# The last attention group in two halves, a seventh buffer of exponentials, two kinds of small work moved between VectorE and GpSimd, and a new order for all of it

## The chip, the cores and the metric

The kernel runs on one core of one Trainium2 chip. The metric is device microseconds (us) from the first to the last instruction, with some 1.7 us that the profiled span leaves out. Each run below was compared with the kernel before on the same chip, in the same rounds. The sets of runs (s1 to s4, s5 to s7, s8 to s11, s12) stood on four chips, so kernels of different sets are compared only through their ratios to the kernel before. One program gives times some 0.3% apart from run to run, and sometimes more.

## The reference, cut to what matters

```python
def reference(A_x, A_wqkv, A_wo, B_x, B_w1, B_w2, B_w3, B_w4):
    def _A_ref(x, wqkv, wo):                       # 2048 rows, 640 columns, 32 heads of 20
        ...
        scores = jnp.einsum("bhqd,bhkd->bhqk", q, k) * (Dh ** -0.5)
        p = _softmax(scores, axis=-1)
        o = jnp.einsum("bhqk,bhkd->bhqd", p, v)
        return ... @ wo
    def _B_ref(x, w1, w2, w3, w4):                 # layernorm, gelu, shifts, two MLP stages
        ...
    xn = _layernorm(A_x)
    s = _A_ref(xn, A_wqkv, A_wo)
    g = _silu(_B_ref(xn, B_w1, B_w2, B_w3, B_w4))
    return A_x + s * g
```

The attention needs 32 x 2048 x 2048 exponentials, and they set the time.

## The kernel before

Heads are worked on four at a time, queries 512 at a time: 8 x 4 = 32 groups of 16 key tiles. For two heads and one key tile TensorE makes a 128 x 1024 tile of scores in PSUM, ScalarE takes its exponential into one of six buffers, and TensorE multiplies the buffer with the values into one accumulator bank. Some key tiles go to VectorE instead, which makes their exponentials out of integer operations: an eviction (`fnu`) and "bit pieces". The second branch of the reference (B) is spread between as filler.

```python
    def exp_act(self, hs, sa):
        ...
        self.T("act", c_act(1024),
               lambda e: e.activation(self.PT[:, hp.slot, :], self.psum[...], AF.Exp, scale=cfg.scale),
               reads=[sa], writes=[pa], name=f"exp{self.step}", ..., acq=("PT", hp), rel=hs)
```

At the end of a group VectorE copies the accumulator out, so that the next group may use the bank. The sums of the exponentials go through memory and come back as reciprocals, spread over partitions; then one product finishes the group.

```python
        T("dve", c_dve(512), lambda e: e.tensor_copy(Ob[:, :], self.bank(self.PVB)[:, :]), ...)      # the copy
        ...                                                       # sums to memory and back, reciprocal
        T("sp", C_SP, lambda e: e.dma_start(RB[:, :], ...), ...)  # reciprocals, spread
        T("dve", c_dve(512, "1x"), lambda e: e.tensor_tensor(dst, Ob[:, :], RB[:, :], op=ALU.mult), ...)   # the product
```

`T` does not issue an instruction; it hands one to a planner inside the program. From assumed durations and a table of due times (`DUE`) the planner fixes, before the launch, the order in which each engine works its instructions off. On the chip every engine keeps to that order: when the next instruction's data are late, the engine stands.

## Time and profile before

| | before |
|---|---|
| time, median of 3 runs | 886.55 us |
| span of the profiled run | 884.1 us |
| first exponential | 35.65 us |
| exponentials on ScalarE | 834 |
| gaps of ScalarE from the first to the last exponential | 13.0 us |
| from the end of the last exponential to the end of the span | 11.0 us |
| busy: ScalarE, TensorE, VectorE | 96%, 93%, 81% |

The span is read as a sum along ScalarE: the start, the exponentials at 0.933 us each, 46.5 us of other functions, the gaps, the tail. The lines are in the prediction.

### The profile page before, as it was taken

What the parts mean: (1) busy time and instruction counts of PE and PEld (TensorE: products, weight loads), DVE (VectorE), ACT (ScalarE), POOL (GpSimd) and SP (SyncE); (2) the same over time, 40 slices, a digit from 0 to 9 for tenths busy, and PEclk for the clock granted to TensorE, in tenths of its full rate; (3) what the DMA queues carried; (4) which work ended last, traced back from release to release, by engine and by line L of the source; (5) the groups of instructions that cost most, each with busy time, mean ns of one, the idle gap of its engine ahead of it and who ended that gap; (6) DMA issues with size and microseconds to landing.
All of it is one profiled execution on the core that took longest, in us unless ns stands there. A gap on an engine that the chain in (4) does not pass through costs nothing.

```text
span 884.1 us, 34138 instructions
## 1 busy us (share of the span) xinstructions
PE 822.8 (93%) x15594; PEld 361.9 (41%) x15594; DVE 716.2 (81%) x986; ACT 846.9 (96%) x896; POOL 42.9 (5%) x74
## 2 busy tenths in 40 slices
PE   3899999998999999999999899999999799999996
PEld 2433333333444443433334444443433344444553
DVE  7747797876888889999998657997889794898675
ACT  7799999998999999999999999999999999999994
POOL 9500000000000000000000000000000000010000
PEclk9999999999999999999999999999999999999998
DMA  6002632331210002332122302132221212023322
GB/s 224 10 8 61 137 96 73 95 95 36 52 41 25 26 25 64 90 101 52 47 55 62 113 26 56 54 91 69 56 64 44 70 32 69 24 65 101 114 69 75
DMA packets 86481, 59.01 MB, mean 67 GB/s; under 512 B 53057, under 2 KB 77841, under 8 KB 86337
## 3 DMA queue, kind: packets, MB, share of 16 engines
q1 hardware_dynamic: 86336, 56.82, 23.5%
q8 instruction: 123, 2.02, 0.9%
q14 instruction: 22, 0.17, 0.1%
HBM read 42.10 MB, written 10.63 MB: 60 GB/s over the span
## 4 chain that ended last, share of the span: by engine, by line
ACT 55%; PE 19%; DVE 17%; DMA 5%; POOL 1%; issue 1%; POOLq 0%
ACT arena L1444 53%; PE psum L782 8%; PE psum L1420 6%; DVE arena L1371 5%; DVE arena L1471 4%; DMA arena<-recips 3%; PE psum L1345 2%; PE psum L1388 2%; DMA recips<-arena 2%; PE psum L1380 1%; ACT arena L1809 1%; DVE arena L984 1%; ACT arena L1825 1%; DVE arena L1805 1%; DVE arena L1225 1%
## 5 line engine op out<-in xcount | busy, mean ns | idle before, releaser
L1444 ACT ACTIVATE arena<-psum 128x1024 bf16<-128x1024 f32 x834 | 777.8, 1038 | 14.4 <-PE psum L1420 5.0
L1420 PE MATMUL psum<-arena 128*32 128x512 bf16 x4928 | 375.7, 381 | 8.0 <-ACT arena L1444 6.6
L782 PE MATMUL psum<-arena 128*32 128x320 bf16 (+1 forms) x5952 | 359.8, 333 | 6.8 <-DVE arena L1179 2.8
L1471 DVE TENSOR_SCALAR arena<-psum 128x1024 uint16<-128x1024 f32 (+1 forms) x192 | 231.5, 1206 | 42.1 <-PE psum L1388 41.3
L1371 DVE TENSOR_SCALAR arena<-arena 128x4096 uint16<-128x4096 uint16 (+1 forms) x224 | 231.4, 1059 | 3.6 <-PE psum L1380 2.5
L782 PEld LDWEIGHTS psum<-arena 128*32 128x32 bf16 x5952 | 150.5, 97 | 146.2 <-issue 20.7
L1345 PE MATMUL psum<-arena 128*22 128x512 bf16 x1668 | 161.8, 381 | 1.2 <-DVE arena L1506 0.6
L1420 PEld LDWEIGHTS psum<-arena 128*32 128x32 bf16 x4928 | 104.4, 95 | 137.2 <-ACT arena L1444 95.2
L1380 PE MATMUL psum<-arena 128*22 128x512 bf16 x1520 | 126.5, 380 | 2.5 <-DVE arena L1371 2.2
L1388 PE MATMUL psum<-arena 32*128 32x512 bf16 x816 | 85.4, 384 | 16.6 <-ACT arena L1444 9.7
L1345 PEld LDWEIGHTS psum<-arena 128*22 128x22 bf16 x1668 | 42.5, 92 | 55.8 <-issue 11.8
L1388 PEld LDWEIGHTS psum<-arena 32*128 32x128 bf16 x816 | 21.9, 90 | 102.5 <-ACT arena L1444 81.4
L1380 PEld LDWEIGHTS psum<-arena 128*22 128x22 bf16 x1520 | 35.8, 91 | 44.5 <-issue 9.7
L1805 DVE CAST arena<-psum 128x512 bf16<-128x512 f32 x48 | 32.8, 684 | 8.3 <-PE psum L782 8.1
L1225 DVE CAST arena<-psum 128x512 bf16<-128x512 f32 x40 | 27.3, 682 | 10.9 <-PE psum L782 10.8
L1820 DVE TENSOR_TENSOR arena<-psum,arena 128x320 bf16<-128x320 f32 x32 | 15.6, 486 | 22.0 <-PE psum L782 22.0
L1590 DVE SCALAR_TENSOR_TENSOR arena<-psum,arena 128x320 bf16<-128x320 f32 x32 | 15.6, 489 | 19.0 <-PE psum L782 18.9
L1519 DVE TENSOR_TENSOR arena<-arena 128x512 bf16<-128x512 f32 x28 | 19.2, 686 | 11.5 <-DMA arena<-recips 11.4
L984 DVE BATCH_NORM_STATS2 arena<-arena 128x6 f32<-128x320 bf16 x52 | 23.0, 480 | 2.2 <-DMA arena<-in_A_x_dram 2.2
L1286 DVE CAST arena<-psum 128x320 bf16<-128x320 f32 x32 | 15.4, 488 | 10.9 <-PE psum L782 10.5
L1506 DVE COPY arena<-psum 128x512 f32<-128x512 f32 x28 | 19.2, 685 | 3.5 <-PE psum L1345 2.3
L1089 PE MATMUL psum<-arena 128*32 128x128 bf16 x320 | 8.9, 248 | 13.7 <-DVE arena L999 13.1
(103 smaller groups left out, 283.8 us busy)
## 6 DMA issues: line engine op xcount, KB each, us to landing
arena<-in_B_w_dram SPq DMA_DIRECT2D x48, 160.0 KB, 2.6
arena<-recips SPq DMA_DIRECT2D x28, 256.0 KB
arena<-arena SPq DMA_DIRECT2D x124, 32.0 KB, 1.9
arena<-in_B_w_dram SPq DMA_DIRECT2D x4, 960.0 KB, 6.0
arena<-in_A_x_dram SPq DMA_DIRECT2D x8, 320.0 KB, 5.3
arena<-in_A_x_dram SPq DMA_DIRECT2D x16, 160.0 KB, 2.3
out_dram<-arena SPq DMA_DIRECT2D x16, 160.0 KB, 1.8
heads<-arena SPq DMA_DIRECT2D x112, 20.0 KB
```

The costliest lines, as they stand in the source:

```text
L782: ins = e.matmul(pb[32 * c:32 * c + 32, 0:N], lhsT(k, c), rhs(k, c), start=(k == 0), stop=(stop and k == nk - 1), tile_position=(0, 32 * c))
L984: lambda e, li=li, n=n, hh=hh: e.bn_stats(st[:, li, 6 * hh:6 * hh + 6], xn[:, n, hD * hh:hD * hh + hD]),
L1225: T("dve", c_dve(512), lambda e, h=h, c=c: e.tensor_copy(KS[:, 512 * c:512 * c + 512], self.wbank(h)[:, 0:512]), reads=[wa], writes=[A("KS ...
L1345: ins = e.matmul(pb[32 * i:32 * i + 22, 0:512], VA[:, ql, kts[x // 2], i, :], PT[:, slots[x // 2][0].slot, 512 * (x % 2):512 * (x % 2) + 512],
L1371: T("dve", c_dve(w, "4x"), lambda e, v=v, dst=dst: e.tensor_scalar(dst, U[:, ub, 0:w], 0.5, EXP_B[v], op0=ALU.mult, op1=ALU.add), reads=ha ...
L1380: ins = e.matmul(pb[32 * i:32 * i + 22, 0:512], wv, dst[:, at:at + 512].bitcast(BF16), start=first, stop=final, tile_position=(0, 32 * i))
L1388: return e.matmul(out, self.KT[32 * i:32 * i + 32, b, 128 * kt:128 * kt + 128], self.QT[32 * i:32 * i + 32, b, 512 * qc:512 * qc + 512], s ...
L1420: ins = e.matmul(out[32 * c:32 * c + 32, :], self.KT[:, b, 128 * kt + 32 * c:128 * kt + 32 * c + 32], self.QM[:, gb, 2 * a + jj, :], start ...
L1444: lambda e: e.activation(self.PT[:, hp.slot, :], self.psum[:, 512 * hs.slot:512 * hs.slot + 1024], AF.Exp, scale=cfg.scale),
L1471: ins = e.tensor_scalar(U[:, ub, 1024 * at + 512 * k:1024 * at + 512 * k + w], self.psum[:, 512 * hd.slots[k]:512 * hd.slots[k] + w], a_ex ...
L1506: T("dve", c_dve(512), lambda e: e.tensor_copy(Ob[:, :], self.bank(self.PVB)[:, :]), writes=[("PV", 0), A("Ob")], name=f"ob{quad}_{qc}", c ...
L1805: T("dve", c_dve(512), lambda e, h=h, fc=fc, i=i: e.tensor_copy(GT[:, i, fc, :], self.wbank(h)[:, 0:512]), reads=[wa], writes=at, name=f"g ...
```

## The change

The change means to shorten three of these terms. The last group is cut into two halves of 256 queries, so that the first half can be finished beside the second. A seventh buffer lets ScalarE run further ahead of TensorE; it is paid for with one of the seven buffers (`RR`) of branch B. The product goes to GpSimd, so that VectorE no longer waits for the reciprocals, and three clears go from GpSimd to VectorE. With these the table of due times, the number of key tiles for VectorE in each group and the assumed time of several operations were searched anew, and four normalisations left GpSimd.

```diff
-            k0=100.3, k1=-164.3, k2=-87.4, k3=-108.7, k4=-66.2, v0=-24.5, v0s=-0.38, ...
+            k0=-95.4, k1=-178.8, k2=-94.5, k3=-123.5, k4=-127.1, v0=-33.6, v0s=-0.77, ...
...
-        self.POOLN = [1, 9, 13, 15]
+        self.POOLN = []
...
+        self.ONP = 1
+        self.LAST = [[[4, 1]], []]
         self.ND = (
...
-            pl.pool("PT", 6)
+            pl.pool("PT", 7)
...
-        T("pool", 3000, lambda e: e.memset(self.QM[:, :, :, :], 0.0), ...)
+        T("dve", c_dve(4096, "4x"), lambda e: e.memset(self.QM[:, :, :, :], 0.0), ..., due=-40000.0)
...   (the same for KT and QT)
+            if last and qc == NQC - 1:
+                for half in range(2):
+                    self.last_half(quad, qc, half, gb)
...   (last_half: 256 queries, an accumulator of its own)
-        T("dve", c_dve(512, "1x"), lambda e: e.tensor_tensor(dst, Ob[:, :], RB[:, :], op=ALU.mult),
+        T("pool" if cfg.ONP else "dve", 1500 if cfg.ONP else c_dve(512, "1x"), lambda e: e.tensor_tensor(dst, Ob[:, :], RB[:, :], op=ALU.mult),
...
-        self.RR = self.alloc("RR", [7, 512], FP32)
+        self.RR = self.alloc("RR", [6, 512], FP32)
```

## The prediction

> **What bounds the kernel now.** I read the page first (shares of the span), then the groups of instructions by shape, then ScalarE's own timeline over the whole span, then the waits, and last the start and the end row by row. The page gives ACT 96%, PE 93%, DVE 81%, Pool 5%. ScalarE's work is almost all one group:
>
> ```profile
> L1444 ACT ACTIVATE arena<-psum 128x1024 bf16<-128x1024 f32 x834 | 777.8, 1038 | 14.4 <-PE psum L1420 5.0
> ...
> L1519 DVE TENSOR_TENSOR arena<-arena 128x512 bf16<-128x512 f32 x28 | 19.2, 686 | 11.5 <-DMA arena<-recips 11.4
> ```
>
> 834 exponentials took 777.8 us, so one costs 0.933 us of pace (its record of 1038 ns overlaps the next). The second row is the product that the change moves: 19.2 us of work, and 11.4 us in which VectorE stood still until the reciprocals had come back by DMA.
>
> ScalarE's timeline cuts the span in three. First, 35.65 us until the first exponential. Then 837.4 us up to the end of the last one at about 873.06: 777.8 of exponentials, 46.5 of other functions and table loads (Gelu 8.74 + 2 x 10.44, six loads of 1.28, eight Tanh at a pace of 1.15), and 13.0 of gaps, added up from the bracketed idle times. Last, 11.0 us of tail. So time goes by the count of exponentials, the gaps and the two ends. The largest gaps, in ScalarE's timeline, with the VectorE rows of the same moments from VectorE's timeline:
>
> ```profile
> 207.21 0.69 DVE L1519 TENSOR_TENSOR arena<-arena 128x512 bf16<-128x512 f32 x1 [2.86 <-DMA arena<-recips]
> ...
> 209.62 1.02 ACT L1444 ACTIVATE arena<-psum 128x1024 bf16<-128x1024 f32 x1 [2.18 <-PE psum L1388]
> ...
> 452.74 29.18 ACT L1444 ACTIVATE arena<-psum 128x1024 bf16<-128x1024 f32 x31 [1.79 <-PE psum L1345]
> ...
> 565.19 0.68 DVE L1519 TENSOR_TENSOR arena<-arena 128x512 bf16<-128x512 f32 x1
> ...
> 565.91 0.69 DVE L1506 COPY arena<-psum 128x512 f32<-128x512 f32 x1
> ...
> 567.16 2.86 ACT L1444 ACTIVATE arena<-psum 128x1024 bf16<-128x1024 f32 x3 [1.65 <-PE psum L1345]
> ```
>
> The reader is to see that the product stands in VectorE's queue ahead of the copy that frees the accumulator bank (L1506) or of the PSUM evictions. When it waits 2.86 us for a DMA, ScalarE loses 2.18 us soon after, and 2.33 more in seven small gaps up to 224. At 452 and 567 the wait is on L1345, the product with the values, which gives an exponential's buffer back. The waits by engine say the same in total:
>
> ```profile
> ACT arena L1444 <- PE psum L1345: 4.8, 6, 1.8
> ```
>
> The start, from the timeline of 31 to 34.5 us:
>
> ```profile
> 31.69 2.15 POOL L951 MEMSET arena<- 128x2048 bf16 x1
> 31.72 2.15 DVE L1166 TENSOR_SCALAR arena<-arena 128x4 bf16<-128x4 f32 x1
> 33.93 0.10 PEld L1140 LDWEIGHTS psum<-arena 128*32 128x32 bf16 x4 [2.02 <-DVE arena L1166]
> ```
>
> A VectorE instruction on four columns lasts exactly as long as GpSimd's clear beside it; the like one on six columns (L1181) takes 0.24 us elsewhere. It stands on the chain to the first exponential, so some 1.9 us are lost to a clear. Earlier GpSimd holds that chain itself: the clear of QM (L926, 4.52 to 8.03) and a normalisation of 2.57 us from 9.35 stand before the powers that release the first tiles. The tail is a pure chain:
>
> ```profile
> 874.00 0.72 DVE L1493 STREAM_TRANSPOSE arena<-psum 128x512 f32<-128x512 f32 x1 [0.49 <-PE psum L1380]
> ...
> 877.04 1.56 DVE L1609 SCALAR_TENSOR_TENSOR arena<-psum,arena 128x640 bf16<-128x640 f32 x2 [0.56 <-PE psum L1602]
> ...
> 880.92 0.96 DVE L1650 TENSOR_TENSOR arena<-arena 128x640 bf16<-128x640 bf16 x2
> ```
>
> **What the Trainium skill says.** "SBUF — State Buffer", section "SBUF: two separate sides": VectorE's second port pair is GpSimd's, an exclusive lock held for a whole instruction by a two-port VectorE instruction or a GpSimd one. The trace agrees: the pair of rows at 31.7. "GPSIMD Engine Reference", section 3.1: a two-input float32 product over 2048 elements takes 4497 ns there against 2293 on VectorE. A quarter of that, with its fixed part, is an estimate of 1.2 to 1.5 us for our 512; the trace has no such GpSimd row. "VectorE: DVE Perf Modes", section "Zero memsets can be issued as uint32 (trn2)": a memset takes one cycle per element whatever the type. This matters, because the change plans its clears on VectorE at the fast rate, a quarter of that. The trace shows only GpSimd's: 4096 elements in 3.51 us, 0.86 ns each. "Perfetto Trace Analysis", section "Optimization Strategy": repeated bubbles on the saturated engine can mean too few buffers. The L1345 waits agree.
>
> **The change part by part.**
>
> Count of exponentials. A group has 32 tiles, less two for each block given to VectorE. The old table sums to 95 blocks: 1024 - 190 = 834, as the page counts. In the new one the first 31 groups have 96 blocks: 992 - 192 = 800. The last group now runs as two halves of 256 queries, with one key tile of the first half on VectorE: 15 + 16 = 31. Total 831, three fewer: 3 x 0.933 = -2.8 us. VectorE evicts 193 tiles where it evicted 190, some 4 us more for it, beside other work.
>
> Gaps. With the product on GpSimd, VectorE neither waits for the DMA nor spends 0.6 us before the copy. The cluster of 209 to 224 (2.18 + 2.33 = 4.5 us) should shrink to about 1. A seventh buffer lets ScalarE run one exponential, 0.93 us, further ahead, and the copy comes 0.6 to 0.7 us sooner, so the gaps at 452 and 567 (3.44 together) should leave about 0.5. The other 5.1 us are scattered waits for scores (L1420) that nothing here removes; the retuned due times may move them either way, and I take 4.5. Gaps 13.0 to 6.0: -7.0 us.
>
> The product's price on GpSimd: 28 times 1.2 to 1.5 us with the lock. The bit pieces (L1371) use two ports and are busy 231 of 884 us, so some products must meet one. If each costs VectorE 0.4 us on average, that is 11 us, against 19.2 + 11.4 freed. VectorE has 19% free, so I count nothing on the path.
>
> The start. GpSimd loses 3.5 + 1.8 + 2.15 us of clears and four normalisations. On the path that frees the 1.9 us at 31.7, and up to about 3 us in the first powers. Against it stand 8192 elements of clears at the head of VectorE's queue. At one cycle per element of 0.96 GHz (the same page) that is an estimate of 8.5 us, from 1.5 to 10, where the first statistics now start at 3.68: some 5.4 us of VectorE's work move back. VectorE is busy 24.5 of the first 31 us, so not all of this is absorbed. ScalarE takes one more transposed tile (0.55) and two normalisations (0.85 each). I take the first exponential at 34.2 us: -1.5, the least certain term.
>
> The tail. From the last exponential: four products with the values in place of twelve, 0.95 to 0.4 us. Transpose, reciprocal, product, transpose on 256 columns instead of 512: each row has about 0.69 us over 512, half of its length gone, so 2.5 to 1.6. TensorE 0.5 as before. Two tiles to evict and add (0.78 + 0.45 each) instead of four: 4.85 to 2.5. The store stays at 2.2. Sum 11.0 to 7.2: -3.8 us. The first half's closing work falls beside the second half's exponentials. A score tile is 16 matmuls of 256 columns instead of 8 of 512, the same columns, so the pace should stay 0.93.
>
> Sum: -2.8 - 7.0 - 1.5 - 3.8 = -15.1 us. 886.55 - 15.1 = 871.4; I say 871.5.
>
> **The rivals.** First, TensorE becomes the bound: it is busy 93%, and from 855 to 872 the chain runs through it without a break. Then removed ScalarE gaps come back as waits for scores and the 7 us shrink to about 2: 876.5. Against it: ScalarE ran 54 to 138 and 696 to 802 without a gap under the same load. Second, the lock bites: GpSimd's products delay bit pieces and with them the PSUM banks for scores. If 28 products cost ScalarE 0.3 us each, 8 us come back: about 880. Against it: VectorE's idle share. Third, the start: full-rate clears at VectorE's head could make it later by 2 us (875); or, if they run fast and are hidden before the first data, it gains 4 (869). Fourth, the retuned order is simply better, leaving gaps near 3 us: 868, just beyond 2%.
>
> **Range and chances.** The end of the tail and the count are sure to about 1 us, the gaps to 4, the start to 3; together about 5 us one way. 8 times in 10: 865 to 878. The line of 2% is 868.8, which needs two of the doubtful terms to go well: 0.27. Slower by 2% would need the lock far beyond my worst sum: 0.01.
>
> **What would show it.** Right: 831 exponentials at 0.93 us; L1519's successor a GpSimd row of 1.2 to 1.5 us x28, with no VectorE wait on the reciprocals; gaps between exponentials near 6 us; waits of ScalarE on the product with the values near 1 us in place of 4.8; first exponential near 34 us with VectorE's clears ending near 10; tail near 7 us. Wrong: bit pieces much longer than 1.22 us on average (the lock), gaps that stay at 13 under another releaser (TensorE), a first exponential after 36, or pauses over 1 us in the last group, where VectorE and ScalarE share two score slots.

## The result, and the profile after

The changed kernel took 884.16 us (median of 4 runs, 883.71 to 886.75), the kernel before 886.37 in the same rounds. The ratio is 0.9983, with a 95% interval of 0.9963 to 1.0003: the same. A ratio here and below is taken from the fast runs of both kernels in the same rounds, so it is not quite the ratio of the medians quoted. The predicted 871.5 and its range were missed on the slow side.

The sum along ScalarE, from the two profiles. The gaps are all idle times of ScalarE between first and last exponential, small ones too (added up again in this way, before has 12.9).

| | before | predicted | after |
|---|---|---|---|
| first exponential, us | 35.65 | 34.2 | 39.66 |
| exponentials | 834 | 831 | 831 |
| gaps, us | 12.9 | 6.0 | 12.1 |
| tail, us | 11.0 | 7.2 | 9.1 |
| span, us | 884.1 | | 882.0 |

The four differences are +4.0, -2.8 (three exponentials at 0.933), -0.8 and -1.9. Their sum, -1.5, is the measured -2.1 to within 0.6. The groups of the changed kernel (line, engine, operation, shapes, count; then busy us, mean ns; then idle time before and its main releaser):

```profile
L1526 ACT ACTIVATE arena<-psum 128x1024 bf16<-128x1024 f32 x831 | 775.0, 1037 | 13.2 <-PE psum L1349 6.3
...
L1601 POOL TENSOR_TENSOR arena<-arena 128x512 bf16<-128x512 f32 x28 | 37.3, 1332 | 575.7 <-DMA arena<-recips 575.6
```

The parts of the change are there as planned. The product takes 1.33 us on GpSimd, which waits 575.7 us for reciprocals at no cost, and VectorE's 11.4 us of such waits are gone. Yet ScalarE waits as long as before, and L1349, the product with the values that gives a buffer back, is its main releaser at 6.3 us where it was 4.8 (the waits by engine name these two). The clears, from VectorE's timeline (start us, length us, engine, line, operation; in brackets the idle time before it and what ended it):

```profile
1.28 1.76 DVE L930 MEMSET arena<- 128x2048 uint32 x1 [1.28 <-PEq L1939]
3.21 0.91 DVE L954 MEMSET arena<- 128x1024 uint32 x1 [0.16 <-issue]
4.28 0.91 DVE L955 MEMSET arena<- 128x1024 uint32 x1 [0.16 <-issue]
```

They went out as words of four bytes and end at 5.2 us, not near 10. The start is late for another reason, which ScalarE's and TensorE's timelines show:

```profile
39.66 5.61 ACT L1526 ACTIVATE arena<-psum 128x1024 bf16<-128x1024 f32 x6 [0.61 <-PE psum L1484]
```

```profile
17.10 4.01 PE L785 MATMUL psum<-arena 128*32 128x320 bf16 x60
```

The 60 matmuls of 320 columns are tiles of the V projection, which the new due times (`v0`, `v0s`) put ahead of the remaining transposes and the key projection. In the kernel before, V matmuls at this place came 20 at a time between transposes. Eleven V tiles are cast on VectorE before the first exponential, seven in the kernel before. From 17 us on TensorE is busy without a break until 33 us, so whatever stands first pushes the rest back.

New gaps stand in the middle, none of which the kernel before had. ScalarE's timeline at three of them:

```profile
123.61 1.94 ACT L1526 ACTIVATE arena<-psum 128x1024 bf16<-128x1024 f32 x2 [0.99 <-PE psum L1349]
...
163.12 2.85 ACT L1526 ACTIVATE arena<-psum 128x1024 bf16<-128x1024 f32 x3 [1.74 <-PE psum L1349]
...
394.46 2.10 ACT L1526 ACTIVATE arena<-psum 128x1024 bf16<-128x1024 f32 x2 [2.10 <-PE psum L1502]
```

VectorE and TensorE at the first two, from their timelines:

```profile
121.29 1.22 DVE L1553 TENSOR_SCALAR arena<-psum 128x1024 uint16<-128x1024 f32 x1 [0.70 <-PE psum L1484]
122.43 0.68 DVE L1588 COPY arena<-psum 128x512 f32<-128x512 f32 x1
...
161.53 0.76 DVE L1196 TENSOR_SCALAR arena<-arena 128x1024 uint16<-128x1024 uint16 x2 [2.23 <-DMA queries<-arena]
```

```profile
123.16 0.83 PE L1349 MATMUL psum<-arena 128*22 128x512 bf16 x12
...
162.02 0.39 PE L1202 MATMUL psum<-arena 128*32 128x512 bf16 x2 [1.72 <-DVE arena L1196]
```

At 121 VectorE stood idle for 0.70 us, then evicted a score tile, and only then did the copy of the accumulator (L1588). The group's last matmuls had ended by 120.14 in TensorE's timeline, so the copy could have gone into the idle time. Three key tiles of the next group (x12) had waited for it with full buffers, and ScalarE stood for 0.99 us. A gap of this kind stands at the end of four groups (0.99, 0.97, 0.94 and 0.96 us), and one of 0.79 early in the last group. At 161 VectorE stands in its order before data of a transfer, TensorE in its own behind VectorE, and ScalarE loses 1.74. At 394 TensorE waits 2.13 us for a weight tile. These seven gaps make 8.5 us.

The tail, in TensorE's and VectorE's timelines:

```profile
872.67 0.45 PE L1688 MATMUL psum<-arena 128*32 128x320 bf16 x8
```

```profile
873.31 0.81 DVE L1695 SCALAR_TENSOR_TENSOR arena<-psum,arena 128x640 bf16<-128x640 f32 x1
...
875.58 0.82 DVE L1695 SCALAR_TENSOR_TENSOR arena<-psum,arena 128x640 bf16<-128x640 f32 x1
```

The first half's own output matmuls (the row at 872.67) come only when the scores are used up, though its part of VectorE's work had ended by 865.3: they need a score slot, and in the plan scores go first. So its two evictions of 0.8 us and two additions of 0.45 lie in the tail, between the second half's four steps, with one more addition that is left over from the queries before.

### The profile page after: what moved, and what is told of

It reads as the page before. It is cut to its first block, busy times and chain, and to the rows that moved or that the text cites. A ratio compares the mean times of both kernels' runs of the same rounds, so it can differ in the third digit from the quotient of the medians.

```text
span 882.0 us, 34813 instructions
## 1 busy us (share of the span) xinstructions
PE 822.8 (93%) x15922; PEld 371.6 (42%) x15922; DVE 711.8 (81%) x974; ACT 846.0 (96%) x896; POOL 65.9 (7%) x96
## 4 chain that ended last, share of the span: by engine, by line
ACT 45%; PE 34%; DVE 17%; DMA 2%; issue 1%; DVEq 0%
ACT arena L1526 43%; PE psum L785 14%; PE psum L1502 8%; DVE arena L1467 5%; DVE arena L1553 5%; PE psum L1349 3%; PE psum L1484 3%; PE psum L1476 3%; PE psum L1390 2%; DVE arena L988 1%; DMA arena<-in_B_w_dram 1%; ACT arena L1896 1%; DVE arena L1853 1%; ACT arena L1912 1%; DMA queries<-arena 1%
## 5 line engine op out<-in xcount | busy, mean ns | idle before, releaser
L1502 PE MATMUL psum<-arena 128*32 128x512 bf16 x4640 | 352.8, 380 | 7.9 <-ACT arena L1526 6.2
L1553 DVE TENSOR_SCALAR arena<-psum 128x1024 uint16<-128x1024 f32 (+1 forms) x195 | 234.3, 1203 | 50.0 <-PE psum L1484 49.1
L1467 DVE TENSOR_SCALAR arena<-arena 128x4096 uint16<-128x4096 uint16 (+1 forms) x224 | 239.8, 1096 | 2.6 <-PE psum L1476 1.5
L785 PEld LDWEIGHTS psum<-arena 128*32 128x32 bf16 x5952 | 149.6, 97 | 143.1 <-issue 27.4
L1502 PEld LDWEIGHTS psum<-arena 128*32 128x32 bf16 x4640 | 99.0, 95 | 132.4 <-ACT arena L1526 94.0
L1349 PE MATMUL psum<-arena 128*22 128x512 bf16 x1600 | 152.2, 380 | 1.4 <-DVE arena L1588 0.6
L1476 PE MATMUL psum<-arena 128*22 128x512 bf16 x1536 | 128.6, 380 | 2.8 <-DVE arena L1467 2.6
L1601 POOL TENSOR_TENSOR arena<-arena 128x512 bf16<-128x512 f32 x28 | 37.3, 1332 | 575.7 <-DMA arena<-recips 575.6
L1349 PEld LDWEIGHTS psum<-arena 128*22 128x22 bf16 x1600 | 40.1, 92 | 51.8 <-issue 9.1
L1094 PE MATMUL psum<-arena 128*32 128x128 bf16 x320 | 9.1, 245 | 14.1 <-DVE arena L1003 13.5
L1588 DVE COPY arena<-psum 128x512 f32<-128x512 f32 x28 | 19.2, 684 | 2.9 <-PE psum L1349 2.3
```

The costliest lines, as they stand in the source:

```text
L785: ins = e.matmul(pb[32 * c:32 * c + 32, 0:N], lhsT(k, c), rhs(k, c), start=(k == 0), stop=(stop and k == nk - 1), tile_position=(0, 32 * c))
L1349: ins = e.matmul(pb[32 * i:32 * i + 22, 0:512], VA[:, ql, kts[i // 2], i, :], PT[:, slots[i // 2][0].slot, 512 * (i % 2):512 * (i % 2) + 512],
L1467: T("dve", c_dve(w, "4x"), lambda e, v=v, dst=dst: e.tensor_scalar(dst, U[:, ub, 0:w], 0.5, EXP_B[v], op0=ALU.mult, op1=ALU.add), reads=ha ...
L1476: ins = e.matmul(pb[32 * i:32 * i + 22, 0:512], wv, dst[:, at:at + 512].bitcast(BF16), start=first, stop=final, tile_position=(0, 32 * i))
L1502: ins = e.matmul(out[32 * c:32 * c + 32, :], self.KT[:, b, 128 * kt + 32 * c:128 * kt + 32 * c + 32], self.QM[:, gb, 2 * a + jj, :], start ...
L1553: ins = e.tensor_scalar(U[:, ub, 1024 * at + 512 * k:1024 * at + 512 * k + w], self.psum[:, 512 * hd.slots[k]:512 * hd.slots[k] + w], a_ex ...
```

## The experiments

My theory: the parts do what the prediction said, and the new order spends it, at the start, at ends of groups, and where an engine stands in its order before a transfer. The rival: TensorE, at 93%, bounds the kernel, so no order ends much sooner. A third possibility is that one of the parts does nothing. A fourth was not tested: the kernel before never got an order made in the way of s12, so the runs can't say how much of s12's gain needs the parts of the change.

A planner makes such experiments delicate: undo one part, and it finds a quite different order. So each experiment adds a step to the program, after the planner, that keeps every engine's order as it was planned, except for the instructions named, and recomputes the waits. All results were correct.

### s1: the opening in the order of before

```diff
+START = "... all instructions that the plan of before starts ahead of 33 us, in its order ..."
+    order[e] = [clears first, then START's] + [the others as they were]
```

> The changed kernel; only the order of the opening on each engine is that of the kernel before (every instruction that stood ahead of 33 us in the plan of before); the clears stay on VectorE, ahead of all. The changed kernel's first exponential started at 39.66 us, that of before at 35.65. Theory (the new order of the opening, V projection and second query tile ahead of the key projection on TensorE, costs 4.0 us): first exponential at 35 to 37 us, and the time 2 to 4 us under the changed kernel's 884.2. Rival (the clears ahead of the statistics cost it): first exponential stays at 39 to 40 us and the time at 884. Third way: it starts early, and the V tiles that are now behind the first scores give the 4 us back as gaps: time at 884 with more waits for TensorE before 60 us.

890.02 us, ratio to before 1.0037 (1.0017 to 1.0056). The first exponential came at 37.26, and then:

```profile
38.68 4.88 PE L922 MATMUL psum<-arena 128*32 128x320 bf16 x120
```

```profile
43.92 1.94 ACT L1665 ACTIVATE arena<-psum 128x1024 bf16<-128x1024 f32 x2 [3.80 <-PE psum L1623]
```

The V tiles left over now stood in one row of 120 between two scores, and ScalarE waited 3.80 us. It was the third way, and worse than I had put it (884). My seam was bad: the order behind the 33 us was made for an opening in which these tiles were done. The run shows that the old order starts the first exponential sooner, but not what it is worth.

### s2: the clears back on GpSimd

```diff
-        T("dve", ...memset(self.QM...  (and KT, QT)
+        same order, but on GpSimd: QM's ahead of the powers of the first statistics, KT's and QT's at 17 us
```

> The changed kernel with the three clears back on GpSimd (as in the kernel before), every other instruction in the order of the changed kernel. Theory (clears on VectorE cost 3.6 us at its head, which are caught up by 17 us): first exponential within 1 us of 39.7, or later because GpSimd now does the 3.5 us and 2 x 2 us clears ahead of what VectorE waits for; time 884 to 886. Rival (the clears cost the opening 4 us): first exponential at 36 us, time 880.

885.91 us, ratio 0.9992 (0.9968 to 1.0016), first exponential 40.98. As the theory had it: the clears on VectorE are not what makes the start late. (On GpSimd they made it 1.3 us later still.)

### s3: the product back on VectorE

```diff
+    for t in products:            # 28 of them
+        t.eng = "dve"             # where in time it stood on GpSimd
```

> The changed kernel with the 28 products back on VectorE, each at the place in VectorE's order where the product started on GpSimd; all else in the same order. Theory (GpSimd takes a wait off VectorE, 28 products of 0.6 us plus waits for the reciprocals' transfer): VectorE gets 28 x 0.6 = 17 us more work and waits for reciprocals of several us, ScalarE's gaps grow from 12 by 3 to 10 us, time 887 to 894. Rival (the product's place was late enough, nothing depended on it; the lock of the shared port cost VectorE as much as it saved): time within 1 us of 884.2.

888.65 us, ratio 1.0015 (0.9998 to 1.0033), against 0.9983 and 0.9996 for the changed kernel in its two comparisons. So the product on GpSimd is worth some 0.2 to 0.3%, 2 to 3 us, at the low end of what I expected, and with intervals that overlap. VectorE waited little for reciprocals; from its waits (total us, times, longest):

```profile
DVE arena L1709 <- DMA arena<-recips: 2.6, 2, 1.4
```

The new order places the product later than the old one did, so 2.6 us are left of the old 11.4 even on VectorE. The gaps in this profile are 18.2 us, but s8 will show that 17.0 can occur without any change.

### s4: six buffers

```diff
-            pl.pool("PT", 7)
+            pl.pool("PT", 6)       # five products with the values one place ahead
```

> The changed kernel with six buffers of exponentials in place of seven, all else in the same order (five products with V move one place ahead on TensorE, because the order would otherwise never end with six). Theory (the seventh buffer lets ScalarE run ahead where TensorE takes the products late): ScalarE waits for buffers, gaps grow from 12 us by 5 to 15 us, time 889 to 899. Rival (the seventh buffer is hardly ever in use): within 1 us of 884.2.

904.23 us, ratio 1.0193 (1.0168 to 1.0217), slower than I expected; gaps 31.8 us. The group of exponentials says where:

```profile
L1629 ACT ACTIVATE arena<-psum 128x1024 bf16<-128x1024 f32 x831 | 777.4, 1035 | 33.2 <-PE psum L1452 18.3
```

L1452 is the product with the values: ScalarE waited 18.3 us for buffers. The seventh buffer is in use. But this order was made for seven; it does not follow that a seventh would have given the old order 18 us.

### s5: the kernel before, with the product on GpSimd alone

```diff
-        T("dve", ... tensor_tensor(dst, Ob, RB, op=ALU.mult)      # kernel before
+        same order, on GpSimd
```

> The kernel BEFORE with one part of the change alone: its 28 products of the sums with their reciprocals on GpSimd, each at the place in GpSimd's order that its time on VectorE gives; everything else in the order of before, six buffers, old opening, old last group. Theory of the prediction (VectorE's waits for the reciprocals make ScalarE's gaps; GpSimd takes them away): VectorE's waits for reciprocals fall to nothing, ScalarE's gaps from 12.9 us to about 6 to 9, time 4 to 7 us under before. Rival (a gap at a group's end is made by the evictions and by the order that TensorE was given, whoever does the product): gaps stay at 11 to 13 us, time within 1.5 us of before.

885.07 us, ratio 0.9982 (0.9955 to 1.0009). Gaps 11.3 us. This lies between theory and rival; by the interval, the product's move is worth anything from 4 us gained to 1 lost here. No wait of VectorE for reciprocals is left, and the cluster of 209 to 224 us of the prediction is down to 0.8 us in rows of 0.23 and less. The two gaps that the prediction put down to the product's place ahead of the copy, 1.79 at 452 and 1.65 at 567, are still there with 1.27 and 1.81: that reading was wrong. And a gap of 2.37 us stood at 491, where before had 0.71, and one of 1.37 at 658. The first is not the move's doing: s10, with the product on VectorE, has 2.81 at the same place. The price on VectorE, from the groups by shape (the bit pieces):

```profile
L1490 DVE TENSOR_SCALAR arena<-arena 128x4096 uint16<-128x4096 uint16 x156 | 189.7, 1239 | 2.7 <-PE psum L1499 2.0
L1490 DVE TENSOR_SCALAR arena<-arena 128x2048 uint16<-128x2048 uint16 x68 | 48.8, 751 | 1.1 <-PE psum L1499 0.8
```

The counts are those of before, where these took 186.9 and 44.5 us: 7.1 us more for 28 products, 0.25 each. s3 shows it from the other side: its pieces took 191.7 and 41.9 us where the changed kernel's took 195.0 and 44.8, so 6.2 us less.

### s6: the last group undivided

```diff
-            if last and qc == NQC - 1:      # two halves
+            if False:                       # and two key tiles for VectorE, as before
```

> The changed kernel with the last group as before (undivided, two key tiles on VectorE, so 828 exponentials), all instructions up to 834 us in the order of the changed kernel. Prediction's theory (halves are worth 3.8 us of tail): tail 11 to 12 us in place of 9.1, but 3 exponentials (2.8 us) fewer, so the time 0.5 us under to 1.5 us over the changed kernel's 884.2. Rival (the halves are worth their tail in full): 2 to 4 us slower than the changed kernel.

887.99 us, ratio 1.0015 (0.9969 to 1.0061). The tail was 13.6 us, 4.5 more than in halves, and there were 3 exponentials (2.8 us) fewer: 1.7 us in favour of the halves by the profile, 2 to 3 us by the ratios, with a wide interval; that is nearer to the rival than to the theory. But the undivided group had a tail of only 11.0 us in the kernel before. The other 2.6 us come from this run's own order, in which 84 output matmuls of other queries (873.01 to 876.08 us) stand ahead of the last products with the values. Against the tail of before, the halves gained 1.9 us and paid 2.8 for three more exponentials in the last group. So it is not shown that they give anything.

### s7: two stalls mended by hand

```diff
+    later({"sh1_0", "sh1_1", "shev1"}, 2600.0)   # the query bound at 162 us
+    later({"w3_0_11_0"}, 1500.0)                 # the weight tile at 393 us
```

> The changed kernel with two places of TensorE's order mended, where it stood 2.2 and 2.1 us for data that a transfer had not brought (the query bound at 162 us, the weight tile at 393 us): these instructions go 2 to 3 scores later in TensorE's order; all else in the same order. Theory (ScalarE's 1.75 and 2.1 us gaps there come from TensorE standing in order): both gaps go below 0.7 us, gaps in all from 12 to 8.5 to 9.5 us, time 2 to 3.5 us under the changed kernel. Rival (TensorE is the bound around there, the time shows up at the next place): gap sum and time as they were.

884.47 us, ratio 0.9975 (0.9938 to 1.0013): no difference from the changed kernel that these runs can show. The gap at 162 is gone, that at 393 is 1.29 in place of 2.10, and the gaps in all were 14.8 in the profiled run, with new ones of 0.55 to 0.70 at 96, 565 and 590. The four runs were 881.67, 882.1, 886.83 and 886.89, and the profile is that of the slowest. A hand that mends two places of one profile mends too little.

### s8: the changed kernel again

No edit.

> The changed kernel itself, unaltered, as a control on this chip and to see how far its own opening and gaps vary from run to run. In two runs with an opening of the same instructions the first exponential started at 39.66 and at 38.37 us, because TensorE's matmuls of the V projection took 4.0 and 2.6 us for the same 60. Expected: time 883 to 887, first exponential 38 to 40 us, gaps 11 to 16 us.

884.57 us (882.45 to 887.9), ratio 0.9996 (0.9977 to 1.0015): the change is worth nothing that can be told from none on this chip, and 0.17% in the first comparison. The profile fell on the slowest run: 38.53 us to the first exponential and 17.0 us of gaps, against 39.66 and 12.1 with the same instructions in the same order. Three differences can be read off. VectorE and TensorE at the largest new group of gaps:

```profile
94.47 0.69 DVE L1821 TENSOR_TENSOR arena<-psum,arena 128x512 bf16<-128x512 f32 x1 [2.59 <-DMA arena<-rstd]
```

```profile
96.35 0.40 PE L1484 MATMUL psum<-arena 32*128 32x512 bf16 x4 [2.07 <-DVE arena L1553]
```

VectorE stood 2.59 us for a transfer that had come in time in the first profile, the eviction behind it came late, TensorE stood 2.07 for the slot, and ScalarE lost 2.84 us in three gaps. Second, a single gap of 2.44 at 480, where the first profile had 0.34; s1, s6 and s9 have 1.98 to 3.18 at this place, and no run here explains it. Third, the start:

```profile
17.09 2.81 PE L785 MATMUL psum<-arena 128*32 128x320 bf16 x60
```

The same 60 matmuls as in the first profile, from 17.09 to the next row at 19.73: 44 ns each, where they took 64 (17.10 to 20.94). Later in both profiles such a matmul takes 34 ns. "TensorE: Matmul & The Clock Gate", part 1, says that TensorE starts at half its clock and gets the full one after a busy window of some 3.4 us, and that the window runs freely, so that the moment differs from run to run. The trace agrees: 65 ns in the slow stretch and 34 after it in the kernel before (20 matmuls from 17.18 to 18.48, 16 from 20.09 to 20.64), and an end of the slow stretch that moved by over a microsecond between two runs of one program.

### s9 and s10: TensorE warmed with matmuls of zeros

```diff
+            for _ in range(26):       # 10 in the kernel before
+                ins = e.matmul(self.wbank(hw)[:, 0:512], self.QM[:, 0, 0, 0:128], self.QM[:, 0, 1, :], start=True, stop=True)
```

> The changed kernel with 26 matmuls of zeros (512 columns, a result that nothing reads) ahead of all others on TensorE, from the clear at 3.0 us on; all else in its order. Theory (the first matmuls run at half rate until TensorE has been busy some microseconds, and the new order puts 12 V tiles and the second query tile ahead of the key projection, so it pays more of the slow stretch than the old one): the 60 V matmuls at 17 us take 2.6 us or less from their start[...], first exponential at 36 to 37.5 us, time 1.5 to 3 us under the control s8. Rival (the opening waits for the loads and VectorE, TensorE's rate does not matter): first exponential within 0.7 us of the control, time within 1 us.

> The kernel before with 10 such matmuls of zeros, from its clear at 8.0 us on. Theory (the old order pays less of the slow stretch): first exponential 0.5 to 1.2 us earlier than 35.65, so the gap between the two kernels' first exponentials falls from 4.0 to 1.5 to 2.5 us. Rival (both gain alike): the old opening gains as much as the new one in s9.

887.66 us, ratio 1.0036 (1.0014 to 1.0057), and 887.79 us, ratio 1.0033 (1.0016 to 1.0049): both slower, and both misses. In s9 the 26 matmuls ran from 3.10 to 10.46 us, but the 60 V matmuls then still took 57 ns each (17.10 to 20.54). Between lie pauses of 1.90 and 1.39 us and short transposes, and they let TensorE fall back. In s10 the slow stretch lasted longer than before: 20 V matmuls from 18.70 took 1.33 us where they took 0.87. So the runs do not say what a fast TensorE would be worth at the start. Why both kernels lost some 3 us is open.

### s11: another opening

```diff
+HEAD = {"pe": ..., "act": ..., "dve": ..., "pool": ...}     # the order up to the 42nd exponential
+    order[e] = head + [x for x in order[e] if x not in set(head)]
```

> The changed kernel with another order of the opening on the four engines (found by re-timing orders with TensorE at half rate until 18 to 21 us; nothing after exponential 100 is moved; no warming matmuls). It puts only V tiles 0 to 6 ahead of the first score, as before did. Theory (the 4.0 us are the order's): first exponential at 35 to 36.5 us, no gap over 1 us before 60 us, time 2 to 3.5 us under the control s8. Rival (TensorE's work up to exponential 60 is what bounds, so what starts earlier is given back as gaps, as in s1): time within 1 us of the control, gaps before 100 us of 2 to 4 us.

882.52 us, ratio 0.9969 (0.9949 to 0.9988), 2.1 us under s8 on the same chip, at the edge of what six runs of each can tell. The first exponential:

```profile
35.42 8.51 ACT L1695 ACTIVATE arena<-psum 128x1024 bf16<-128x1024 f32 x9 [0.49 <-PE psum L1653]
```

Four gaps of 0.29 to 0.52 before 60 us make 1.6 us together. So the theory holds for the start: the same work on the same engines starts 3 to 4 us sooner in another order and gives back 1.6. TensorE's slow stretch was no shorter here (24 V matmuls from 21.51 to 22.97 us took 61 ns each), so this was not the draw of a fast TensorE. The middle, whose order is that of the changed kernel, kept its gaps (0.99 at 120, 1.62 at 159, 2.01 at 391).

### s12: the whole order, made for late transfers

```diff
+ORDER = (...)     # every engine's list, by name
+        order[e] = [ids[n] for n in names]
```

Here swaps of neighbours were judged by two re-timings with TensorE slow until 19.5 us, one with transfers as planned and one with every transfer 1.2 us late. These served to find an order; the chip judged it.

> The changed kernel, the same instructions and buffers, in an order of all engines found by re-timing swaps with TensorE slow until 19.5 us and, in a second re-timing, every transfer 1.2 us late. Theory (the change does free what the prediction said, and its order gave it away: 4 us at the start, 4.7 us in five places where a group's copy or first products come late, 4 to 9 us where an engine stands in order for a transfer that is late in some runs): first exponential at 35 to 36.5 us, gaps between exponentials 6 to 9 us in place of 12 to 17, tail 7.5 to 9.5, time 874 to 879, under s11 by 3 us or more and with a smaller spread. Rival (TensorE, 93% busy, is the bound, so any order ends near 882): gaps stay at 12 or more under other releasers, time 881 to 885.

877.99 us (876.15 to 878.84), ratio to before 0.9902 (0.9877 to 0.9926). Same instructions, same buffers, same engines as in the changed kernel. That is some 1%, clear of the noise. The profiles of the table are single draws: those of after and s12 fell on the fastest run of each, that of s8 on the slowest.

| | after | after again (s8) | s11 | s12 |
|---|---|---|---|---|
| first exponential, us | 39.66 | 38.53 | 35.42 | 35.33 |
| gaps, us | 12.1 | 17.0 | 14.1 | 8.6 |
| tail, us | 9.1 | 9.1 | 9.1 | 8.7 |
| span, us | 882.0 | 886.2 | 880.4 | 874.4 |

ScalarE's timeline after the place of the gap of 0.99 us (where gaps of 0.18 and 0.23 are left), and VectorE's:

```profile
122.69 47.49 ACT L1798 ACTIVATE arena<-psum 128x1024 bf16<-128x1024 f32 x51 [0.23 <-PE psum L1774]
```

```profile
118.10 0.68 DVE L1860 COPY arena<-psum 128x512 f32<-128x512 f32 x1
118.90 1.22 DVE L1825 TENSOR_SCALAR arena<-psum 128x1024 uint16<-128x1024 f32 x1
```

The copy now goes ahead of the eviction. The long row shows 51 exponentials without a pause, across 162 us, where the transfer of the queries cost 1.74. ScalarE's wait for the product with the values:

```profile
ACT arena L1798 <- PE psum L1621: 1.3, 2, 1.0
```

It is 1.3 us where it was 4.8 before and 6.3 after; the prediction had said near 1. TensorE is now busy for 830.8 us, 95%. The rival, that TensorE holds any order at 882, falls. s12 beats both kernels, the changed one only through the ratios (0.9902 against 0.9983 and 0.9996).

## Why the prediction was wrong

**Exponentials, -2.8: right.** 831 at 0.933 us. The sum hid that the last group has three more of them (31 for 28) and the others six fewer.

**The product's price: right in kind, too high.** 1.33 us each, inside the estimate of 1.2 to 1.5. The bit pieces gave the lock away as foreseen, but with 6 to 7 us, not 11. It cost ScalarE nothing that a run shows: in s3 and in s5 the kernel with the product on GpSimd is the faster by the medians. (The page's figure from which the estimate came is that of an addition, not a product.)

**Gaps, 13.0 to 6.0: the step that failed.** It stood in the prediction as "the retuned due times may move them either way, and I take 4.5". The gaps stayed at 12.1 us (17.0 in s8). Those it named did go: in the first profile after, there is no gap over 0.31 between 164 and 256, and none above 0.34 from 400 to 780. In their place stand seven new ones that make 8.5 us, made by the order and not by the parts. s12 shows it, with the same parts and 8.6 us of gaps in all; five of the seven are gone there, and two are left (0.96 and 0.74). A part of the error sits in the reading of the profile before: the cluster at 207 was the work of one late transfer (2.86 us of VectorE's wait). In s10, with the product on VectorE as before, the wait at that place was 1.27 us and the gap 0.59; at 368 it was 2.11 us, and the gaps there 3.2 us in place of 0.67. I took the draw of one run for a fixed cost. What was drawn is the place: VectorE's waits for reciprocals in all were 11.4 us before and 11.7 in s10. By s5 the product's move is worth some 2 us on the old order, not 4 to 7, with an interval that reaches 4.

**Start, -1.5: wrong, +4.0 (+2.9 in s8's profile).** The price of the clears was one error: estimated at 8.5 us, they took 3.6. It would have helped, and s2 shows that they do not matter. The working had the engines' queues in the order of before and let the change only take from or add to them. That the new due times alone reorder TensorE's queue (eleven V tiles and the second query tile ahead of the first exponential) was not looked at. s11 shows that order to cost 3 to 4 us at the first exponential and 2 us in time.

**Tail, -3.8: right in kind, mis-sized at -1.9.** The term that failed is "The first half's closing work falls beside the second half's exponentials". Two evictions (1.63 us) and two additions (0.90) of it lie in the tail, though partly in VectorE's waits, and one addition (0.45) of the queries before. The pace of 0.93 in the last group, another doubt, held: 28 exponentials took 26.0 us without a gap.

**The rivals.** The first (TensorE's waits take the place of the gaps, 876.5) had the right symptom and the wrong cause, as s12 shows. The fourth, "the retuned order is simply better", was given as a chance; its opposite was not in the list, and that is what happened. The runs do not settle all of it. Product (s3, s5: 2 to 3 us gained) against the opening (s11: 2 us lost) leaves 0 to -1 us by an estimate from these runs; the halves add -2 to -3 by s6, or cost 0.9 against the tail of before. -2.2 and -0.5 were measured (medians); with run-to-run differences of 2 us the rest cannot be told. What a seventh buffer gives the old order was not tried and stays open: the change paid for it with one `RR` buffer, and with six of these the order of branch B would have had to change too. (That it does not fit beside seven of them is not shown by a run here.)

## What to carry to other kernels

Where a planner fixes each engine's order, a change of parts is also a change of the order, and the order can be worth as much as the parts: here 0.8 to 0.9% of the time without touching an instruction (0.9902 over 0.9983 and over 0.9996). Predict such a change by asking for the new order first, and read the gaps from several profiles, since those behind a late transfer are a draw. An order judged with late transfers as well as timely ones was faster and, in these runs, spread less (2.7 us against 5.5 in s8); that it was the late transfers that made it better, and not the search as such, was not tested.

## What the Trainium skill lacked or had wrong

- "VectorE: DVE Perf Modes", "Zero memsets can be issued as uint32 (trn2)": right about the form, and I misread it as something the author must do. A clear of bf16 written as such went out as uint32 by itself, 1.76 us for 4096 elements and 0.91 for 2048, where GpSimd took 3.51 us for the 4096. The page doesn't say that it happens unasked. Its pace of one cycle per element is slower than measured: the two lengths (2048 and 1024 words) put a word at 0.83 ns, where a cycle at the page's 0.96 GHz is 1.04.
- "SBUF — State Buffer", "SBUF: two separate sides": right about the lock; it gives no price. Here 28 GpSimd products of 1.33 us cost VectorE's bit pieces 6 to 7 us, and a VectorE instruction of 0.24 us beside a clear became 2.15 us before the change.
- "GPSIMD Engine Reference", section 3.1: its addition of 2048 elements, scaled to a product of 512 elements, did well (estimate 1.2 to 1.5 us, measured 1.33 and 1.42).
- "TensorE: Matmul & The Clock Gate", part 1: right about the slow start (65 against 34 ns a matmul) and its varying end. It gives no length for pauses shorter than its idle window that bring the slow state back; in s9 pauses of 1.90 and 1.39 us with short matmuls between were enough. And the granted clock that the profile shows read full speed in the slow stretch (1.00 from 17 to 21 us in the changed kernel), so here the state must be read from the matmuls.
- No page that I read has how much one program's transfers differ from run to run: the same wait was 0 and 2.59 us, or 2.86 and 1.27 us.
